# LSH attention and a gated mixing layer on one core: a new order of the instructions, one sign operation in the first batch, V's sums on two engines

## The chip, the core and the metric

The kernel runs on one core of a Trainium2 chip. The core has TensorE (PE, with PEld for its weight loads), VectorE (DVE), ScalarE (ACT), GpSimd (POOL) and SyncE (SP, which only issues DMAs here). Each engine runs its own list of instructions strictly in order and waits on semaphores for the others. The metric is the device time of one execution in microseconds (us), as a median over runs.

## What is computed

Four batches of eight heads, 768 tokens, head width 64. A 6-bit hash of each query and key (signs of a projection) masks the scores; softmax and PV follow. The heads' outputs, side by side, are the input `x` (768 x 512 per batch) of a mixing layer.

```
q_bits = (einsum(q, proj) > 0); k_bits = (einsum(k, proj) > 0)
mask = bucket(q_bits)[:, None] == bucket(k_bits)[None, :]
attn = softmax(where(mask, q @ k.T / 8, -1e9))        # per batch and head
x = concat over heads of attn @ v                     # 4 x 768 x 512
theta = x @ w_theta
y = w_tok_r @ (x * cos(theta)) + w_tok_i @ (x * sin(theta))
u = x + y
out = u + relu(u @ w_ch)
```

## The kernel before

Operands are split into a high and a low 16-bit float half, so that one product is three fp16 matmuls. Heads are loaded in pairs (`prep_qk`, `prep_v`), four pairs per batch.

**Queries and keys.** `bits` multiplies both heads' q and k by the projection into one PSUM bank `pb` of 128 rows; `sign` turns it on VectorE into the tile `rows`; DMAs (`assemble`) carry the halves `hl` and the `rows` into the matmul operand `qk` of the next head. For the very first head the pieces are copied by engines or DMAs one by one (`piece`). The 18 KB or 9 KB DMAs of `rows` and the 1.5 KB DMA of `row` stand in SyncE's one list with all loads.

**A head.** Score matmuls `sq` go to PSUM; VectorE takes row maxima (`mc`, then `mx`); TensorE transposes them (`pmx`), once per head and twice for the first head; VectorE makes `row` and `fl` of it, and DMAs put these into `qk` and into a flag tile `ft`. Then `st` matmuls (scores, transposed), exponentials `pf` on ScalarE, halves `p1` (ScalarE or GpSimd) and `p2` (GpSimd), and the PV matmuls `po`. Odd heads of batches 2 and 3 go another way (`bt`, `bm`, `late`).

**V.** `prep_v` scales V into halves (`vv`) and sums its six token blocks on GpSimd, in three instructions (`s1`, `s2`, in place in `vb`); a small matmul `pm` makes the mean of it.

**The mixing layer.** `ps_th` (theta), sines on ScalarE, the products `f` and halves `z` (VectorE, ScalarE, GpSimd), the token product `py`, then `s_u`, `ps_r`, and the store. The weights are prepared on the chip in the first 250 us (`wf_th`, `wf_ch`, `wf_t`), mostly on VectorE and ScalarE.

**The order.** Every step is an `op` with its alternatives by engine. The order of all ops, and the engine of each, is a table of numbers (`ORDER`, some 4,000 entries like `P2k`: letter = engine, rest = number of the op), and `SLOTS` says which of the rotating buffers each takes. `issue_all` writes them out in this order; so the table sets what each engine runs, one after the other.

**Beats.** 22 ops `beat` of two matmuls each on a constant flag tile keep TensorE busy in the first 22 us; their results are not used.

Of the kernel before, what the change touches and what calls it, by code (L numbers as in the profile page):

```python
# [11 lines left out]
F16 = mybir.dt.float16  # L12
F32 = mybir.dt.float32
# [19 lines left out]
def lsh_attention_moe_kernel(ctx: ExitStack, tc: tile.TileContext, q, k, v, proj, w_theta, w_tok_r, w_tok_i, w_ch, out):  # L33
# [6 lines left out]
    P = 128  # L40
# [27 lines left out]
    one33 = const.tile([P, 33], F16, name="one33")  # L68
    DVE.memset(one33, 1.0)
    ones1 = ones[:, :33]  # L70
# [8 lines left out]
    DVE.memset(fts[1], 1.0 / 1024)  # L79
# [25 lines left out]
    FREE = dict(ft=2, mc=2, hl=2, rows=2, sc=2, nat=2, vv=2, x=2, z0=1, z1=1, wx=1, wz=1, wf=1, xt=2, xd=2, vw=2, **BUFS)  # L105
# [28 lines left out]
    def on(e, dur, fn):  # L134
        return {e: (dur, fn)}
# [120 lines left out]
    def prep_weight(src, dst, nm, n, tag, stage, prio, step, by=1.0):  # L256
# [94 lines left out]
    def prep_v(b, hp, prio):  # L351
        t = {}
        full = t["full"] = [b == 0 and (hp, j) in FULL for j in range(2)]
        onpe = False
# [45 lines left out]
        def s1():  # L400
            POOL.tensor_tensor(t["vb"][:, :, 0:3], t["vb"][:, :, 0:3], t["vb"][:, :, 3:6], ALU.add)

        def s2():
            for n in (1, 2):
                POOL.tensor_tensor(t["vb"][:, :, 0], t["vb"][:, :, 0], t["vb"][:, :, n], ALU.add)

        def mean():
            t["pm"] = pm = bank(sm_, [33, 2, D], f"pm_{b}_{hp}")
            if onpe:
                first = True  # L410
                for j in range(2):
                    if full[j]:
                        for n in range(T):
                            mm(pm[:, j], ones1, t["vw"][j][:, n, :D], first, n == T - 1)
                            first = False
                if n_:
                    js = slice(lo_, lo_ + n_)
                    for n in range(2 * T):
                        c0 = 0 if n < T else W1
                        mm(pm[:, js], one33, t["vv"][:, js, n % T, c0 : c0 + D], first, n == 2 * T - 1)  # L420
                        first = False
            else:
                mm(pm, ones33, t["vb"][:, :, 0], True, True)

        def by(r):
            return 1.0 / S if onpe else sc[r]

        def mh():
            t["mh"] = ap_.tile([33, 2, D], F16, tag=f"mh{sv.idx}", bufs=1, name=f"mh_{b}_{hp}")
            ACT.activation(t["mh"], t["pm"], AF.Copy, scale=by(slice(0, 33)))  # L430
            ACT.activation(t["mt"][0:1, :, :D], t["pm"][0:1], AF.Copy, scale=by(slice(0, 1)))
# [13 lines left out]
        if not onpe:  # L445
            c = op("va1", prio, on("POOL", 970, s1), [c], [svb])
            c = op("va2", prio, on("POOL", 936, s2), [c], [svb])
        d = op("vmean", prio, on("PE", sum(700 if f_ else 380 for f_ in full) if onpe else 220, mean), [c], [svb, sv, sm_] + sw_)
# [184 lines left out]
    def maxima(h, n_, b, G, asm, own=False):  # L633
# [37 lines left out]
        for blk, (lo, hi) in {1: (4, 6), 0: (0, 4)}.items() if own else ((0, (0, T)),):  # L671
            def group(blk=blk, lo=lo, hi=hi):
# [3 lines left out]
                def small(nm_):  # L676
                    return ap_.tile([hi - lo, P], F16, tag=f"{nm_}{lo}_{hi}{smc.tag}", bufs=1, name=f"{nm_}_{nm}_{lo}")
# [638 lines left out]
FOURTHS = ()  # L1316
# [24 lines left out]
    "0000000000000000000000101012021202122001300010000011100100110020001010101103110002111111222033301001011033212201103003130110020311"  # L1341
    "1200111031011101010100011100101010111011132002201003031111030332022010111203032031100131203011010000000033000110011030011001111131"
    "1232103201211010303321211102001031332002021101001311120011101101130000100011130010101001131131100120011113030232020313200332101111"
    "3100311130011020310000000321011000101101111001010010123101000133201131021030012130032112103000103213000213012102320320111300010111"
    "2101010010000111101101010010011313010011213123201200211010113321023020130332112310011010023201031321101010003000021010000011000111"
    "0100012101013123200101323010102320120100113131332112200332010300201132120303201011011131011300111010100111001011013010032013213201"
    "0031000022313320300011101030103203201211102311321011022303000001200013111100011031102331133211000323021101000232102303111001000310"
    "0101200112321023031121110030000111110133010010111020112331111120012230311112300110200133200033032111212102233010121003000013312000"
# [212 lines left out]
```

## Time and profile before

| what | value |
|---|---|
| time, median of 3 runs (lowest, highest) | 689.69 us (689.42, 693.13) |
| the profiled execution: its own time | 687.36 us |
| the profiled execution: span, first to last instruction | 685.6 us |
| busy of the span: PE, DVE, ACT, POOL | 96%, 84%, 78%, 67% |
| granted TensorE clock | 0.999 |

Of the profiled execution 1.8 us lie around the span, and it is 2.3 us below the median of the runs. In the rows, L followed by a number is a line of the kernel before; most matmuls share the helper's line L82, so they are told apart by their tiles. A bracket at the end of a row is the idle time of the engine before it and what ended it.

### The profile page before, as it was taken

To read this page: it belongs to the slowest core of one execution; us is meant where nothing else is said; L and a number is where in the kernel's file an instruction comes from. 1 tells how busy PE (TensorE), PEld (TensorE's weight loads), DVE (VectorE), ACT (ScalarE), POOL (GpSimd) and SP (SyncE) were. 2 spreads that over 40 slices of the span, in tenths; PEclk is the share of its full clock that TensorE was granted. 3 is DMA by queue.
4 is the path that set the end of the run, shared out by engine and by line. 5 is a ranking of instruction groups with operands and counts; after the bars stand their busy time and mean duration, and the time that the engine had idled before them with its cause. 6 is when DMAs were issued, how large, how long until landed. Compare 5 with 4: busy or idle time off the path is not lost.

```text
span 685.6 us, 16806 instructions
## 1 busy us (share of the span) xinstructions
PE 659.5 (96%) x6257; PEld 389.7 (57%) x6257; DVE 579.1 (84%) x1236; ACT 535.8 (78%) x947; POOL 457.7 (67%) x453
## 2 busy tenths in 40 slices
PE   7899989899989999999999999999999999999997
PEld 2487776745544556656445565655645565644454
DVE  6999999999999999899988788889978778688121
ACT  5779989999977799999887889998984588873002
POOL 6838857378537668999568778978755898743012
PEclk9999999999999999999999999999999999999999
DMA  6564867677266452579537788989754685880113
GB/s 242 142 170 130 206 165 199 188 156 175 77 170 157 97 111 68 130 197 177 113 82 139 152 167 172 181 210 189 119 105 62 138 173 103 139 177 17 32 29 109
DMA packets 176985, 95.39 MB, mean 139 GB/s; under 512 B 149024, under 2 KB 166792, under 8 KB 176904
## 3 DMA queue, kind: packets, MB, share of 16 engines
q1 hardware_dynamic: 176760, 94.30, 61.4%
q8 instruction: 49, 0.80, 0.5%
q14 instruction: 32, 0.26, 0.2%
q10 hardware_dynamic: 144, 0.03, 0.0%
HBM read 32.53 MB, written 6.29 MB: 57 GB/s over the span
## 4 chain that ended last, share of the span: by engine, by line
PE 64%; DVE 23%; issue 5%; DMA 4%; ACT 2%; POOL 1%; SPq 0%; POOLq 0%; DVEq 0%; ACTq 0%
PE py L82 19%; PE po L82 13%; PE st L82 9%; PE ps_r L82 7%; DVE mc L660 6%; PE ps_th L82 6%; PE sq L82 4%; PE bt L82 4%; DVE f L1164 2%; DMA qk<-row 2%; DVE hl L498 1%; PE pb L82 1%; DVE z L1175 1%; DVE wf_t L244 1%; DVE wf_t L326 1%
## 5 line engine op out<-in xcount | busy, mean ns | idle before, releaser
L764 POOL TENSOR_TENSOR p<-pf,p 128x512 f16<-128x512 f32 x180 | 233.1, 1309 | 73.3 <-ACT p L758 62.9
L82 PE MATMUL py<-z,wtk 128*128 128x512 f16 (+1 forms) x900 | 206.6, 370 | 0.4 <-DVE mt L434 0.2
L660 DVE TENSOR_REDUCE mc<-sq 128x1 f32<-128x512 f32 (+1 forms) x216 | 143.2, 681 | 19.5 <-PE sq L82 18.3
L752 ACT ACTIVATE pf<-st 128x512 f32<-128x512 f32 x216 | 124.9, 592 | 22.0 <-PE st L82 17.5
L82 PEld LDWEIGHTS <-qk 108*128 108x128 f16 (+2 forms) x1056 | 96.1, 99 | 77.7 <-issue 17.7
L82 PEld LDWEIGHTS <-wtk 128*128 128x128 f16 x900 | 85.6, 97 | 89.8 <-issue 3.7
L82 PE MATMUL st<-qk 108*128 108x256 f16 (+1 forms) x576 | 124.9, 326 | 3.9 <-DMA qk<-row 2.3
L918 POOL TENSOR_TENSOR late<-pf,late 128x384 f16<-128x384 f32 x96 | 93.2, 985 | 25.2 <-ACT late L912 20.5
L82 PEld LDWEIGHTS <-p 128*128 128x128 f16 x2160 | 85.7, 97 | 21.5 <-issue 2.5
L758 ACT ACTIVATE p<-pf 128x512 f16<-128x512 f32 x148 | 90.7, 626 | 6.7 <-PE po L82 5.6
L82 PE MATMUL po<-vv,p 128*128 128x65 f16 (+1 forms) x2160 | 93.3, 193 | 0.1
L82 PE MATMUL sq<-qk 108*128 108x256 f16 (+1 forms) x288 | 78.5, 325 | 8.3 <-DVE mc L660 4.0
L904 ACT ACTIVATE pf<-bt,bm 128x384 f32<-128x384 f32 x96 | 60.7, 665 | 21.1 <-DVE bm L892 16.8
L82 PE MATMUL ps_th<-wth,t_x 128*128 128x512 f16 x288 | 68.2, 379 | 1.4 <-DVE z L1130 0.8
L82 PE MATMUL ps_r<-wch,t_u 128*128 128x512 f16 x276 | 68.9, 379 | 0.3 <-DVE wch L298 0.3
L876 DVE TENSOR_REDUCE bm<-bt 128x1 f32<-128x384 f32 x96 | 50.4, 549 | 11.2 <-PE bt L82 10.6
L1218 ACT ACTIVATE rl<-ps_r,qu 128x512 f32<-128x512 f32 x23 | 15.7, 683 | 46.8 <-PE ps_r L82 37.2
L82 PEld LDWEIGHTS <-t_x 128*128 128x128 f16 x288 | 27.4, 97 | 33.0 <-DMA t_x<-s_x 1.8
L1221 POOL TENSOR_TENSOR x<-rl,x 128x512 f32<-128x512 f32 (+1 forms) x9 | 12.0, 1328 | 48.2 <-DVE s_u L1020 32.7
L82 PE MATMUL bt<-qk 108*128 108x384 f16 x192 | 43.3, 327 | 0.0
L82 PEld LDWEIGHTS <-t_u 128*128 128x128 f16 x276 | 25.4, 97 | 26.8 <-issue 1.6
L1164 DVE SCALAR_TENSOR_TENSOR f<-x,zsc,z 128x512 f32<-128x512 f32 x48 | 38.8, 833 | 1.2 <-POOL z L1175 1.1
(177 smaller groups left out, 1084.0 us busy)
## 6 DMA issues: line engine op xcount, KB each, us to landing
qk<-hl SPq DMA_DIRECT2D x62, 192.0 KB
raw<-in_q_dram SPq DMA_DIRECT2D x16, 384.0 KB
raw<-in_k_dram SPq DMA_DIRECT2D x16, 384.0 KB
vb<-in_v_dram SPq DMA_DIRECT2D x16, 384.0 KB
qk<-hl SPq DMA_DIRECT2D x62, 96.0 KB
out_dram<-x SPq DMA_DIRECT2D x23, 256.0 KB
w_t<-in_moe_w_tok_r_dram SPq DMA_DIRECT2D x6, 768.0 KB
w_t<-in_moe_w_tok_i_dram SPq DMA_DIRECT2D x6, 768.0 KB
```

The source lines that it names most:

```text
L82: PE.matmul(out_, l, r, start=start, stop=stop, skip_group_check=True)
L244: return lambda: eng.tensor_tensor(t["f"][:, part], t["f"][:, part], t["sg"][:, part], ALU.mult)
L660: DVE.tensor_reduce(col()[:, cs], u["sq"], AX.X, ALU.max)
L752: ACT.activation(wide("pf", spf, F32), u["st"], AF.Exp, scale=1.0 / (UNIT * math.sqrt(D)))
L758: ACT.activation(o_, u["pf"], AF.Copy)
L764: return lambda: eng.tensor_tensor(wide("p2", sp2, F16), u["pf"], u["p1"], ALU.subtract)
L876: DVE.tensor_reduce(part(y), w["w"], AX.X, ALU.max)
L904: ACT.activation(w["f"], w["w"], AF.Exp, bias=part(4), scale=part(3))
L918: return lambda: eng.tensor_tensor(dst(1), w["f"], dst(0), ALU.subtract)
L1164: DVE.scalar_tensor_tensor(u["f"], tl[b][:, tt], zsc[:, b : b + 1], t["zw"][r][:, tt], ALU.mult, ALU.mult)
L1218: ACT.activation(v_["r"][:, ds_], r_["ps"][:, ds_], AF.Relu, scale=t["qu"][:, to : to + 1])
L1221: return lambda: eng.tensor_tensor(tl[b][:, to, ds_], v_["r"][:, ds_], tl[b][:, to, ds_], ALU.add)
```

## The change

1. `FOURTHS = (0,)`: in batch 0 `sign` is one instruction over 128 partitions instead of two over 64. Its result lies as 128 rows, so the DMAs that carry it to a head are four of 9 KB (`bits`) instead of two of 18 KB (`pairs`).
2. V's sums are one op with two alternatives: the three GpSimd instructions (`sums`), or one VectorE reduction over a strided view into a new tile `va` (`reduced`). The new table sends eight of the sixteen pairs to VectorE: pairs 1, 2, 3 of batch 1, 0, 1, 3 of batch 2, and 0, 1 of batch 3.
3. The beats read flag tile 1 instead of 0, and the two tiles' first fills change places. Two constants that only these or dead code used are gone; the weights' column totals are a one-pass bf16 matmul.
4. `SLOTS` and `ORDER` are new throughout: the row maxima rotate over three buffers instead of two, and all engines have another order.

```diff
-    DVE.memset(fts[0], 1.0 / 1024)
-    ones = const.tile([P, P], F32, name="ones")
-    DVE.memset(ones, 1.0)
+    DVE.memset(fts[1], 1.0 / 1024)
...
-            mm(tl["pw"], fts[0][:, :P], fts[0][:, :512], True, True)
+            mm(tl["pw"], fts[1][:, :P], fts[1][:, :512], True, True)
...
-            mm(u["pa"], ones, col, True, True)
+            mm(u["pa"], onesb, col.bitcast(BF16)[:, 1:2], True, True)
...
-        def s1():
+        def sums():
             POOL.tensor_tensor(t["vb"][:, :, 0:3], t["vb"][:, :, 0:3], t["vb"][:, :, 3:6], ALU.add)
-
-        def s2():
             for n in (1, 2):
                 POOL.tensor_tensor(t["vb"][:, :, 0], t["vb"][:, :, 0], t["vb"][:, :, n], ALU.add)
 
+        def reduced():
+            t["va"] = ap_.tile([P, 2, D], F32, tag="va" + svb.tag, bufs=1, name=f"va_{b}_{hp}")
+            DVE.tensor_reduce(t["va"], t["vb"].rearrange("p h t d -> p h d t"), AX.X, ALU.add)
...
-            c = op("va1", prio, on("POOL", 970, s1), [c], [svb])
-            c = op("va2", prio, on("POOL", 936, s2), [c], [svb])
+        c = op("va", prio, {"POOL": (1906, sums), "DVE": (860, reduced)}, [c], [svb])
...
-FOURTHS = ()
+FOURTHS = (0,)
...
-S66 S68 P0 So P3 Am S3c Pg S6t Pb A67 Dn P6k A69 D6a D6b Pj D6l P4 P2 D6c S6q A6o Pd G6n D6d D6e D6f Ph D6s S6r A6g Pi Pe D6p A6i P9 D6h Pf
```

What the new table does is seen in the instructions' order. VectorE at the start, up to the first row maxima; `sc` is the scale of the first pair, `rows` the signs, `qk` the first head's operand. Before:

```order
L516 RECIPROCAL sc_0_177<-sc_0_177 128x1
L543 TENSOR_SCALAR rows_0_191<-pb_0_181,pp 64x384 x2
L517 TENSOR_SCALAR sc_0_177<-sc_0_177 128x1
L518 TENSOR_SCALAR sc_0_177<-sc_0_177 128x1
L519 TENSOR_SCALAR sc_0_177<-sc_0_177 128x1
L520 TENSOR_SCALAR sc_0_177<-sc_0_177 128x2
L562 TENSOR_SCALAR qk_141<-raw_0_0_157,sc_0_177 32x768
L562 TENSOR_SCALAR qk_141<-raw_0_0_157,sc_0_177 64x768
L498 SCALAR_TENSOR_TENSOR hl_0_176<-raw_0_0_155,sc_0_177,hl_0_176 128x768
L498 SCALAR_TENSOR_TENSOR hl_0_176<-raw_0_0_157,sc_0_177,hl_0_176 128x768
L660 TENSOR_REDUCE mc_0_237<-sq_0_8_229 128x2
```

After:

```order
L497 TENSOR_SCALAR sc_0_175<-sc_0_175 128x1
L498 TENSOR_SCALAR sc_0_175<-sc_0_175 128x1
L499 TENSOR_SCALAR sc_0_175<-sc_0_175 128x1
L500 TENSOR_SCALAR sc_0_175<-sc_0_175 128x2
L523 TENSOR_SCALAR rows_0_195<-pb_0_177,pp 128x384
L542 TENSOR_SCALAR qk_137<-raw_0_0_153,sc_0_175 32x768
L540 COPY qk_137<-rows_0_195 12x384
L478 SCALAR_TENSOR_TENSOR hl_0_174<-raw_0_0_153,sc_0_175,hl_0_174 128x768
L190 TENSOR_SCALAR vsc<-pa_0_214 128x1
L191 TENSOR_SCALAR vinv<-vsc 128x1
L478 SCALAR_TENSOR_TENSOR hl_0_174<-raw_0_0_151,sc_0_175,hl_0_174 128x768
L640 TENSOR_REDUCE mc_0_238<-sq_0_6_231 128x1
```

The scale no longer stands behind the two sign instructions, one sign remains, and one of the copies of `rows` into the first head's operand is now here (three are on GpSimd, none is a DMA; two were DMAs).

ScalarE at the same place, from the squares of the raw q and k on. Before:

```order
L487 ACTIVATE hl_0_176,sc_0_177<-raw_0_0_157 128x768
L558 ACTIVATE qk_141<-rows_0_191 12x384
L492 ACTIVATE hl_0_176<-raw_0_0_155,sc_0_177 128x768
L492 ACTIVATE hl_0_176<-raw_0_0_157,sc_0_177 128x768
L558 ACTIVATE qk_141<-raw_0_0_155,sc_0_177 64x768
L380 ACTIVATE vv_121,vs_0_227<-vb_0_172 128x12x64
L391 ACTIVATE vw_137<-vb_0_172,vsc 128x6x64
```

After:

```order
L467 ACTIVATE hl_0_174,sc_0_175<-raw_0_0_153 128x768
L374 ACTIVATE vv_117,vs_0_183<-vb_0_158 128x12x64
L472 ACTIVATE hl_0_174<-raw_0_0_151,sc_0_175 128x768
L472 ACTIVATE hl_0_174<-raw_0_0_153,sc_0_175 128x768
L538 ACTIVATE qk_137<-raw_0_0_153,sc_0_175 64x768
L538 ACTIVATE qk_137<-raw_0_0_151,sc_0_175 64x768
L538 ACTIVATE qk_137<-hl_0_174 64x768 x2
L538 ACTIVATE qk_137<-hl_0_174 32x768
L385 ACTIVATE vw_133<-vb_0_158,vsc 128x6x64
```

V's squares moved ahead of the halves (V's load is now the third of SyncE's loads instead of the sixth), and of the first head's operand ScalarE makes five pieces (four of 64 rows, one of 32) instead of three (one of 64 and two smaller, one of them behind these rows).

VectorE in the middle of batch 1, where the first of its V sums stands now (`va`, pair 1 of batch 1); before, this place has no such row and GpSimd has the three instructions:

```order
L640 TENSOR_REDUCE mc_1_2_2574<-sq_1_2_1_2668 128x1
L1110 SCALAR_TENSOR_TENSOR z1_0_2286<-n_0_3_2673,mg_0_2279,ps_th0_3_2588 128x512
L401 TENSOR_REDUCE va_1_1_2698<-vb_1_1_2209 128x128
L640 TENSOR_REDUCE mc_1_2_2574<-sq_1_2_8_2677 128x2
L795 RECIPROCAL rc_1_0_0_2727<-po_1_0_0_2344 128x6
L640 TENSOR_REDUCE mc_1_2_2574<-sq_1_2_7_2691 128x1
```

It now stands between the row maxima of the head that follows.

Counted over the two orders: VectorE's instructions ahead of the maxima that the `pmx` of head 6 of batch 1 (the last of that batch) transposes.

| kind | before | after |
|---|---|---|
| sign, 64 partitions / 128 partitions | 18 / 0 | 10 / 4 |
| V's sums (`va`) | 0 | 3 |
| low half `z` by subtraction, 128x512 (L1175) | 8 | 6 |
| `wf_t` by sign (L244), `wf_ch` by sign, `wf_th` by sign (L250) | 10, 6, 1 | 9, 4, 2 |
| last sum `x<-rl,x` (L1221) | 1 | 0 |
| magnitude `z<-z` (L1133), cast to `z` (L1171) | 2, 2 | 1, 1 |
| `s_x<-x` high half (L1016) | 1 | 2 |
| first head: `qk<-raw` 64x768 (L562), copies into `qk` | 1, 0 | 0, 2 |

All other kinds of VectorE stand ahead of it as often as before (but for two fills). TensorE has 36 `po` matmuls more and two `st` matmuls of 512 columns fewer ahead of this `pmx`. ScalarE's list ahead of the same head's first `p1` has as many instructions as before but for one, partly of other kinds. SyncE has 92 entries instead of 81 ahead of the DMA of `row` for head 5 of batch 0, and 14 more DMAs for `rows` in all. Over the whole program all the work of TensorE is the same; GpSimd casts `p1` or `late` 16 times more and subtracts `z` four times more, and sums V eight times less.

## Rows read from the trace of the kernel before

**Rows 1.** The page: busy time by engine; then the span in 40 equal slices.
```profile
PE 659.5 (96%) x6257; PEld 389.7 (57%) x6257; DVE 579.1 (84%) x1236; ACT 535.8 (78%) x947; POOL 457.7 (67%) x453
PE   7899989899989999999999999999999999999997
DVE  6999999999999999899988788889978778688121
```
**Rows 2.** Windows: stretch in us, its length, busy time of PE, PEld, DVE, ACT, POOL.
```profile
0.00:20.00 20.00, 14.78 (x72) 5.76 (x72) 14.16 (x39) 11.01 (x19) 13.54 (x37) 1.00 0.67 225
20.00:80.20 60.20, 58.45 (x608) 42.22 (x605) 57.08 (x125) 51.13 (x98) 40.85 (x41) 1.00 0.58 155
80.20:180.00 99.80, 92.46 (x922) 61.46 (x921) 97.58 (x197) 93.18 (x159) 67.90 (x56) 1.00 0.70 172
180.00:272.80 92.80, 88.34 (x830) 49.61 (x829) 91.44 (x170) 77.36 (x144) 58.60 (x49) 1.00 0.49 118
272.80:480.00 207.20, 204.84 (x2113) 118.52 (x2112) 182.40 (x415) 185.57 (x339) 169.62 (x165) 1.00 0.76 158
480.00:660.00 180.00, 179.32 (x1574) 97.92 (x1572) 128.98 (x281) 113.31 (x185) 101.21 (x106) 1.00 0.54 101
660.00:685.60 25.60, 21.26 (x150) 14.18 (x147) 7.43 (x14) 4.25 (x8) 5.98 (x5) 0.98 0.33 93
```
**Rows 3.** Timeline of PE: `pmx` of head 5, batch 0, and of head 6, batch 1.
```profile
80.19 0.27 PE L684 MATMUL pmx<-ident,mx 128*6 128x128 f32 x1
...
272.84 0.27 PE L684 MATMUL pmx<-ident,mx 128*6 128x128 f32 x1
```
**Rows 4.** Timeline of all engines from 4 to 14 us: start, length, instruction.
```profile
4.12 0.84 ACT L487 ACTIVATE hl<-raw 128x768 f16<-128x768 f32 x1 [1.66 <-DMA raw<-in_q_dram]
5.83 0.19 ACT L487 ACTIVATION_READ_ACCUMULATOR hl<-raw 128x1 f32 x1
6.19 1.39 DVE L543 TENSOR_SCALAR rows<-pb,pp 64x384 f16<-64x384 f32 x2 [0.75 <-PE pb L82]
7.60 1.71 SPq L556 DMA_DIRECT2D qk<-rows  x2
7.61 0.21 DVE L517 TENSOR_SCALAR sc<-sc 128x1 f32<-128x1 f32 x1
7.96 0.50 POOL L560 COPY qk<-rows 12x384 f16<-12x384 f16 x1
8.23 0.25 DVE L520 TENSOR_SCALAR sc<-sc 128x2 f32<-128x2 f32 x1
8.52 1.76 ACT L492 ACTIVATE hl<-raw,sc 128x768 f16<-128x768 f32 x2 [1.10 <-DVE sc L520]
10.18 0.92 ACT L558 ACTIVATE qk<-raw,sc 64x768 f16<-64x768 f32 x1
12.51 0.87 ACT L380 ACTIVATE vv<-vb 128x768 f16<-128x768 f32 x1 [1.41 <-DMA vb<-in_v_dram]
12.98 0.59 PE L82 MATMUL sq<-qk 108*128 108x256 f16 x3 [2.90 <-DMA qk<-rows]
13.40 1.89 DVE L660 TENSOR_REDUCE mc<-sq 128x2 f32<-128x512 f32 x3 [1.78 <-PE sq L82]
```
**Rows 5.** Groups of DVE by form: line, shapes, count, busy us, mean ns, idle before.
```profile
L660 DVE TENSOR_REDUCE mc<-sq 128x1 f32<-128x512 f32 x144 | 96.9, 682 | 12.6 <-PE sq L82 11.7
L876 DVE TENSOR_REDUCE bm<-bt 128x1 f32<-128x384 f32 x96 | 50.4, 549 | 11.2 <-PE bt L82 10.6
L1175 DVE TENSOR_TENSOR z<-f,z 128x512 f16<-128x512 f32 x32 | 25.8, 824 | 2.4 <-ACT z L1169 1.8 <-POOL z L1171 0.5
L543 DVE TENSOR_SCALAR rows<-pb,pp 64x384 f16<-64x384 f32 x32 | 21.5, 672 | 1.0 <-PE pb L82 0.7
L1221 DVE TENSOR_TENSOR x<-rl,x 128x512 f32<-128x512 f32 x15 | 12.5, 834 | 1.0 <-ACT rl L1218 1.0
L244 DVE TENSOR_TENSOR wf_t<-wf_t 128x768 f32<-128x768 f32 x10 | 11.7, 1175 | 0.0
L231 DVE SCALAR_TENSOR_TENSOR wf_t<-w_t,wf_t 128x1536 uint32<-128x1536 uint32 x6 | 11.0, 1836 | 0.0
L227 DVE TENSOR_SCALAR wf_t<-w_t 128x1536 uint32<-128x1536 uint32 x6 | 5.7, 954 | 0.1
L1016 DVE TENSOR_SCALAR s_x<-x,zsc 128x512 f16<-128x512 f32 x8 | 5.1, 636 | 0.1
L1171 DVE CAST z<-f 128x512 f16<-128x512 f32 x9 | 4.0, 454 | 0.0
L1133 DVE TENSOR_SCALAR z<-z 128x512 uint32<-128x512 uint32 x8 | 4.0, 499 | 0.1
L250 DVE TENSOR_TENSOR wf_ch<-wf_ch,wg_ch 128x256 f32<-128x256 f32 x6 | 2.8, 462 | 0.0
L250 DVE TENSOR_TENSOR wf_th<-wf_th,wg_th 128x512 f32<-128x512 f32 x1 | 0.7, 669 | 0.0
L562 DVE TENSOR_SCALAR qk<-raw,sc 64x768 f16<-64x768 f32 x1 | 0.6, 612 | 0.0
```
**Rows 6.** Chain that ended last, in order of time: start, us, what.
```profile
38.60 0.87 PE st L82 x4
319.70 1.84 PE po L82 x60
```
**Rows 7.** Timeline of SyncE's issues before the `row` of three heads, batch 0.
```profile
41.81 0.36 SPq L481 DMA_DIRECT2D raw<-in_q_dram  x1
44.32 0.72 SPq L695 DMA_DIRECT2D qk<-row  x1
...
52.80 0.41 SPq L209 DMA_DIRECT2D w_ch<-in_moe_w_ch_dram  x1
55.27 0.72 SPq L695 DMA_DIRECT2D qk<-row  x1
...
77.66 2.89 SPq L321 DMA_TRANSPOSE wtk<-wf_t  x1
81.06 0.72 SPq L695 DMA_DIRECT2D qk<-row  x1
```
**Rows 8.** Timeline of PE: the first `st` of head 5, batch 0.
```profile
87.43 0.81 PE L82 MATMUL st<-qk 98*128 98x512 f16 x3 [1.88 <-DMA qk<-row]
```

More of the change, by code (lines that the diff above doesn't have):

```diff
@@ L62, in lsh_attention_moe_kernel @@
     fts = [const.tile([P, S], F16, name=f"ft{n}") for n in range(2)]
-    DVE.memset(fts[0], 1.0 / 1024)
-    ones = const.tile([P, P], F32, name="ones")
-    DVE.memset(ones, 1.0)
+    DVE.memset(fts[1], 1.0 / 1024)
     ones33 = const.tile([P, 33], F32, name="ones33")
     DVE.memset(ones33, 1.0 / S)
-    one33 = const.tile([P, 33], F16, name="one33")
-    DVE.memset(one33, 1.0)
-    ones1 = ones[:, :33]
     onesb = const.tile([P, P], BF16, name="onesb")
@@ L78, in lsh_attention_moe_kernel @@
         DVE.memset(pst[nm], 0.0)
-    DVE.memset(fts[1], 1.0 / 1024)
+    DVE.memset(fts[0], 1.0 / 1024)
     def mm(out_, l, r, start, stop):
@@ L104, in lsh_attention_moe_kernel @@
     phase = "0"
-    FREE = dict(ft=2, mc=2, hl=2, rows=2, sc=2, nat=2, vv=2, x=2, z0=1, z1=1, wx=1, wz=1, wf=1, xt=2, xd=2, vw=2, **BUFS)
+    FREE = dict(ft=2, mc=3, hl=2, rows=2, sc=2, nat=2, vv=2, x=2, z0=1, z1=1, wx=1, wz=1, wf=1, xt=2, xd=2, vw=2, **BUFS)
     def op(name, prio, alts, deps=(), slots=(), table=None):
@@ L398, in low @@
             DVE.scalar_tensor_tensor(t["vf"][:, hs_, W1 : W1 + D], src()[:, hs_], sc, t["vf"][:, hs_, :D], ALU.mult, ALU.subtract)
-        def s1():
+        def sums():
             POOL.tensor_tensor(t["vb"][:, :, 0:3], t["vb"][:, :, 0:3], t["vb"][:, :, 3:6], ALU.add)
-        def s2():
             for n in (1, 2):
                 POOL.tensor_tensor(t["vb"][:, :, 0], t["vb"][:, :, 0], t["vb"][:, :, n], ALU.add)
+        def reduced():
+            t["va"] = ap_.tile([P, 2, D], F32, tag="va" + svb.tag, bufs=1, name=f"va_{b}_{hp}")
+            DVE.tensor_reduce(t["va"], t["vb"].rearrange("p h t d -> p h d t"), AX.X, ALU.add)
         def mean():
             t["pm"] = pm = bank(sm_, [33, 2, D], f"pm_{b}_{hp}")
[L409 to L423, printed above, removed]
+            mm(pm, ones33, t["va"] if "va" in t else t["vb"][:, :, 0], True, True)
         def by(r):
-            return 1.0 / S if onpe else sc[r]
+            return sc[r]
         def mh():
-            t["mh"] = ap_.tile([33, 2, D], F16, tag=f"mh{sv.idx}", bufs=1, name=f"mh_{b}_{hp}")
+            t["mh"] = ap_.tile([33, 2, D], F16, tag="mh", bufs=1, name=f"mh_{b}_{hp}")
             ACT.activation(t["mh"], t["pm"], AF.Copy, scale=by(slice(0, 33)))
@@ L444, in prep_v @@
         c = last_
-        if not onpe:
-            c = op("va1", prio, on("POOL", 970, s1), [c], [svb])
-            c = op("va2", prio, on("POOL", 936, s2), [c], [svb])
-        d = op("vmean", prio, on("PE", sum(700 if f_ else 380 for f_ in full) if onpe else 220, mean), [c], [svb, sv, sm_] + sw_)
+        c = op("va", prio, {"POOL": (1906, sums), "DVE": (860, reduced)}, [c], [svb])
+        d = op("vmean", prio, on("PE", 220, mean), [c], [svb, sv, sm_] + sw_)
         f = op("vmh", prio, on("ACT", 500, mh), [d], [sm_, sv])
@@ L676, in small @@
                 def small(nm_):
-                    return ap_.tile([hi - lo, P], F16, tag=f"{nm_}{lo}_{hi}{smc.tag}", bufs=1, name=f"{nm_}_{nm}_{lo}")
+                    return ap_.tile([hi - lo, P], F16, tag=f"{nm_}{lo}{smc.tag}", bufs=1, name=f"{nm_}_{nm}_{lo}")
                 def both():
@@ L1345 @@
[L1345 to L1348, printed above, removed]
@@ L1497 @@
+P350 P35y A351 P361 A35z G352 D360 P362 P363 P364 S353 P365 A369 P366 P367 P368 D36a A36c G36d S36b S36e
 """
```

302 lines of the change are left out of this document (152 added, 150 removed).

## The prediction, made before the changed kernel ran

> **What bounds the kernel now.** I read the page first. PE is busy for 659.5 of 685.6 us, and its 40 slices are thin only in the first slice and in the first two fifths of the span [rows 1]. Only PE's idle time can change much, since all its matmuls remain. The windows say where that idle lies: 5.2 us in 0 to 20, 1.75 in 20 to 80.2, 7.3 in 80.2 to 180, 4.5 in 180 to 272.8, then 2.4 in the next 207 us, 0.7 in the next 180 and 4.3 in the tail [rows 2]. So 18.8 of the 26.1 us lie ahead of 272.8.
>
> Who is waited for there? From 80.2 to 272.8 DVE is busy for 97.58 + 91.44 = 189.0 of 192.6 us: DVE is the bound of that stretch, PE waits for it. From 20 to 80.2 PE is the bound (58.45 of 60.2). Behind 272.8 PE is within 1.2% of full until the tail. The two markers, the `pmx` of head 5 of batch 0 and of head 6 of batch 1, stand at 80.19 and 272.84 [rows 3]. My model of the time: **when the second marker comes, plus PE's remaining work, which stays as it is**, with the tail unchanged (the order of the last stores is the same in both tables). The second marker comes when DVE has done all that stands ahead of it: 14.16 + 57.08 + 97.58 + 91.44 = 260.3 us of work and 12.5 us of idle [rows 2].
>
> **DVE's work ahead of the second marker.** The counts are those of the table in the section on the change, the durations those of the groups [rows 5].
> - Sign: 18 instructions of 64 partitions become 10 and 4. An instruction's time goes by its 384 elements per partition, so one over 128 partitions is priced as one over 64: 4 x 0.672 = **-2.69**.
> - V's sums: three `va` more. The trace has no reduction of this form. Two contiguous reductions give a slope: 128 elements more cost 682 - 549 = 133 ns, 1.04 ns each, so one of 768 costs 682 + 256 x 1.04 = 0.95 us. Bounds: below, the 0.62 ns per element of L227 (954 ns for 1536, reading every second word), 0.48 us; above, the longest instruction of DVE, 1.84 us (L231). I take 0.95, the nearest row being a reduction: 3 x 0.95 = **+2.84**.
> - `z` by subtraction 2 fewer, -1.65; `wf_t` by sign -1.18; `wf_ch` two fewer and `wf_th` one more, -0.92 + 0.67; last sum -0.83; piece of `qk` -0.61; magnitude -0.50; cast -0.45; `s_x` +0.64. Two new copies into `qk` have no row on DVE; the nearest are GpSimd's 0.50 [rows 4] and DVE's 0.61 for a 64x768 piece: +0.6 for both, 0 to 1.2. Together **-4.2**.
>
> The fills (two more or fewer) stand in front of the first load's end and count nothing; if they did, some 0.3. Sum: -2.69 + 2.84 - 4.2 = **-4.1**. It becomes -3.7 if reductions are counted by their pitch back to back (three in 1.89, 0.63 each [rows 4]), since then `va` costs 0.90 and the others are shorter by similar shares. I take **-4**.
>
> PE has more ahead of the marker: 36 `po` at 1.84/60 = 0.031 us, +1.1, and two `st` fewer at 0.87/4 = 0.218, -0.4 [rows 6]: **+0.7** done early, which is taken from what remains behind it. PE's idle ahead of the marker therefore shrinks by 4.7 in all.
>
> **The start.** Before, the first `sq` waits 2.90 us for a DMA of `rows` and begins at 12.98, the first `mc` at 13.40 [rows 4]. The chain: two signs (6.19, 1.39 us) stand ahead of the scale's steps, which end at 8.48; ScalarE waits 1.10 for them; two DMAs of 1.71 in SyncE's list carry `rows`. After the change the scale's steps follow the read of the squares (6.02) at once. They ran from 7.61 to 8.48 and there is about as much ahead of 7.61 to do, so the scale ends near 7.1; the one sign (0.7) then ends near 7.8, three GpSimd copies (0.50 each) near 9.4. ScalarE makes the halves (1.76 for two) to 8.9 and two pieces (0.92 each) to 10.7. So the first `sq` comes near 10.7, about 2 us earlier (0 to 3). ScalarE now squares V between; if V's load landed later than 7 us, that would stall it, but V is now the third load.
>
> Are these 2 us worth anything? Between 20 and 80 PE is the bound, and DVE has 3.1 us idle there in which it waits for PE [rows 2]. An earlier start moves everything earlier, PE's idle in the first 20 us falls, and the first marker comes earlier; but DVE then still has all its work from 80 on. DVE's own work in the first 80 us falls by 2 too (signs, a piece), so I take DVE's idle ahead of the second marker to stay at 12.5, and allow -0.5 for ScalarE and queue effects that eat a little: **gain 4.7 - 0.5 = 4.2**.
>
> **Edits costed at nothing.** The beats on the other flag tile: PE has nothing else to do in those 20 us (5.2 idle [rows 2]); if their fill came late, they would start later by its length, under 1 us. The bf16 totals are two matmuls in the weights' preparation, under 0.1 us. Three `mc` buffers can only loosen a wait. The eight V sums moved off GpSimd free GpSimd, which is 67% busy [rows 1]; five of the eight stand on DVE behind the second marker, where DVE has 207.2 - 182.4 = 25 us to spare in one window [rows 2].
>
> **The rivals.**
> *More (D).* The earlier start counts too: DVE idles 2 us less ahead of the second marker. Gain 6.2, own time 681.2, median 683.5. For it: DVE's list is what bounds from 80 on. Against: it was PE that bound up to 80.
>
> *Nothing (A): ScalarE takes the bound.* In 80.2 to 180 ScalarE is busy for 93.18 of 99.80 us, DVE for 97.58 [rows 2]: ScalarE has only 4.4 us less to do there. For it: some 3 us of pieces and V's squares have moved into its start, and if it carries that lateness into this stretch, 4.4 - 3 = 1.4 of DVE's 4.7 us count, less with some waiting. Against: its own list up to the marker is as long as before. Gain 0 to 1, median 689 (688 to 690.5).
>
> *Little (B): the strided reduction costs twice as much.* `va` reads six words 256 bytes apart for each sum. At the upper bound of 1.84 us the three cost 5.5 instead of 2.8, gain 1.5, median 688.2. Against: L227 with every second word shows no penalty (0.62 ns per element) [rows 5], but its step is 8 bytes. The Trainium skill, page "SBUF — State Buffer", section "Door 1: The DMA port swizzle (why `[64,N]` ≈ `[32,N]`)", speaks against the change here: SBUF has 16-byte lines, and each access that crosses to a new line pays a penalty. By that rule L227, two hits to a line, would be free, as the trace has it, and `va`, a new line with every word, would not; no row of this trace has such a step.
>
> *Slower (C): SyncE's list.* Four DMAs of `rows` instead of two, and 14 more in all, stand in the one list that also puts `row` into `qk`; two take 1.71 to issue [rows 4], so 14 are 12 us in batch 0, with 11 more entries ahead of the `row` of head 5. Puts now follow the previous issue by 44.32 - 42.17 = 2.1 and 55.27 - 53.21 = 2.1 us, so SyncE waits there; but for head 5 by 81.06 - 80.55 = 0.5 only, behind a 2.89 us transposition [rows 7], and the `st` of that head waits 1.88 for it [rows 8]. If two DMAs more (1.7) land in front of a `row`, that head's `st` is late by up to 1.7. With seven heads: 7 x 1.7 - 4.2 = +7.7 (697.4); with four, +2.6 (692.3). It decides from three heads on (5.1 against 4.2). Against: two of the three heads looked at have 2.1 us of slack.
>
> **How the numbers follow.** The forecast: span 685.6 - 4.2 = 681.4; with 1.8 around it, own time 683.2; the profiled execution lay 2.33 below the median, so the median is **685.5**. Its own range is 683.5 to 687.5: `va` from 0.48 to 1.84 moves the gain from 5.6 to 1.5, the start from 0 to 3 moves it by about a half to each side. Chances: forecast 0.52, D 0.09, A 0.17, B 0.10, C 0.12. A measurement of this kernel can tell some 0.5%, 3.4 us, from no change; the forecast lies at 4.2, so 0.37 of its 0.52 count as faster and 0.15 as the same. Faster: 0.37 + 0.09 = 0.46. Same: 0.15 + A 0.17 + B 0.10 = 0.42. Slower: C, 0.12. The range from 681.5 to 690.5 takes in D, A, B and the forecast's bounds and leaves out C and the far ends.
>
> **What would show it.** The first `sq` near 10.7 us, without a wait on a DMA; `va` at 0.95 us each, 1.8 would be B; `pmx` of head 6 of batch 1 near 268.6, with DVE still idle for about 12.5 us ahead of it (10.5 would be D); the same share of PE behind it. ScalarE idle for under 3 us from 80 to 180 would be A. `st` waits on `row` above 1.9 us in several heads of batch 0 would be C. My forecast is wrong at its base if the time behind the second marker changes: then PE's remaining work was not the constant I take it for, or a wait moved there.

## The result, and the profile after

The changed kernel took 699.65 us (median of four runs, 698.38 to 701.10), the kernel before 690.70 in its four: the ratio is 1.0125 (95% interval 1.0086 to 1.0163). The forecast was 685.5, with a range of 681.5 to 690.5. The profiled execution spans 696.6 us; its own time is 698.38. Each ratio is to executions of the kernel before taken beside that kernel, and leaves out those with a disturbed clock, so it can differ from the quotient of the medians.

The page of the changed kernel: busy time, then two rows of the 40 slices (PE, and the clock that TensorE was granted).

```profile
PE 669.0 (96%) x6255; PEld 394.7 (57%) x6255; DVE 588.3 (84%) x1230; ACT 534.1 (77%) x938; POOL 450.5 (65%) x447
PE   7899999879999999999999999999999999999997
...
PEclk9999969989999999999999999999999999999999
```

PE is busy for 9.5 us more than before [rows 1], for the same matmuls. Slices 6 and 9 have a clock of 0.6 and 0.8. Over the whole profiled execution the mean granted clock is 0.984; the other three runs had 0.977 to 0.980, so they lost more. Four windows of the changed kernel show both places, the pause and what followed (columns as in [rows 2]: the clock is the third number from the end).

```profile
85.50:88.50 3.00, 0.17 (x2) 0.09 (x1) 0.86 (x2) 0.65 (x2) 2.94 (x3) 1.00 1.10 136
...
90.40:103.90 13.50, 13.50 (x57) 10.18 (x56) 7.68 (x12) 7.64 (x13) 4.61 (x4) 0.50 0.37 117
...
145.90:148.40 2.50, 0.14 (x5) 0.04 (x2) 2.50 (x4) 0.98 (x5) 1.45 (x1) 0.97 1.15 190
148.40:155.00 6.60, 6.06 (x30) 3.34 (x30) 6.60 (x10) 5.81 (x10) 5.91 (x4) 0.50 0.72 150
```

Twice PE pauses for nearly 3 us, and at the pause's end or soon after it the clock is at the lower level (1.2 GHz, a granted clock of 0.50), for at least 13.5 and 6.6 us. PE's timeline names what each pause waited for; its first and last row are the two markers of the prediction.

```profile
79.92 0.27 PE L664 MATMUL pmx<-ident,mx 128*6 128x128 f32 x1
...
88.41 0.38 PE L77 MATMUL st<-qk 98*128 98x512 f16 x1 [2.83 <-DMA qk<-row]
...
148.94 0.37 PE L77 MATMUL sq<-qk 108*128 108x256 f16 x1 [2.90 <-DVE mc L640]
...
284.13 0.27 PE L664 MATMUL pmx<-ident,mx 128*6 128x128 f32 x1
```

The first wait stood in the kernel before too, 1.88 us [rows 8], without a fall. SyncE's timeline shows why it grew.

```profile
71.81 3.72 SPq L595 DMA_DIRECT2D qk<-rows  x4
...
77.74 0.38 SPq L204 DMA_DIRECT2D w_t<-in_moe_w_tok_r_dram  x1
78.18 0.41 SPq L204 DMA_DIRECT2D w_t<-in_moe_w_tok_i_dram  x1
78.69 2.96 SPq L316 DMA_TRANSPOSE wtk<-wf_t  x1
81.75 0.71 SPq L675 DMA_DIRECT2D qk<-row  x1
```

Four DMAs of `rows` take 3.72 us of issue where two took 1.71 [rows 4]. The transposition is issued at 78.69 instead of 77.66 and `row` at 81.75 instead of 81.06 [rows 7], though the marker came 0.27 us earlier than before.

The three windows cut at the markers:

```profile
0.00:79.92 79.92, 73.93 (x679) 48.22 (x680) 71.28 (x159) 66.06 (x119) 51.94 (x70) 1.00 0.57 167
79.92:284.13 204.21, 190.50 (x1785) 117.06 (x1782) 189.37 (x362) 170.36 (x300) 128.49 (x108) 0.95 0.60 142
284.13:696.60 412.47, 404.61 (x3802) 229.43 (x3798) 327.65 (x710) 297.68 (x520) 270.12 (x271) 1.00 0.64 129
```

Behind the second marker lie 412.5 us, before 685.6 - 272.84 = 412.8. So the whole loss lies ahead of it, between the two markers: 204.2 us instead of 192.65.

### The profile page after: what moved, and what is told of

Read it like the earlier page. It is cut to its first block, busy times and chain, and to the rows that moved or that the text cites. A ratio compares the mean times of both kernels' runs of the same rounds, so it can differ in the third digit from the quotient of the medians.

```text
span 696.6 us, 16742 instructions
## 1 busy us (share of the span) xinstructions
PE 669.0 (96%) x6255; PEld 394.7 (57%) x6255; DVE 588.3 (84%) x1230; ACT 534.1 (77%) x938; POOL 450.5 (65%) x447
## 4 chain that ended last, share of the span: by engine, by line
PE 65%; DVE 19%; DMA 6%; issue 4%; POOL 2%; ACT 2%; SPq 1%; POOLq 0%; DVEq 0%; ACTq 0%
PE py L77 22%; PE po L77 12%; PE st L77 9%; PE ps_th L77 6%; PE ps_r L77 6%; DVE mc L640 5%; PE sq L77 5%; PE bt L77 3%; DMA late<-late 2%; DMA t_x<-s_x 1%; DVE wf_t L321 1%; POOL late L898 1%; DMA qk<-row 1%; DVE hl L478 1%; DVE f L1144 1%
## 5 line engine op out<-in xcount | busy, mean ns | idle before, releaser
L744 POOL TENSOR_TENSOR p<-pf,p 128x512 f16<-128x512 f32 x180 | 230.2, 1294 | 72.3 <-ACT p L738 60.7
L77 PE MATMUL st<-qk 108*128 108x256 f16 (+1 forms) x576 | 129.0, 335 | 6.1 <-DMA qk<-row 3.0
L898 POOL TENSOR_TENSOR late<-pf,late 128x384 f16<-128x384 f32 x96 | 94.7, 999 | 23.8 <-ACT late L892 21.0
L738 ACT ACTIVATE p<-pf 128x512 f16<-128x512 f32 x142 | 86.9, 625 | 9.8 <-PE po L77 8.2
L77 PE MATMUL po<-vv,p 128*128 128x65 f16 (+1 forms) x2160 | 91.7, 193 | 0.0
L77 PE MATMUL sq<-qk 108*128 108x256 f16 (+1 forms) x288 | 81.1, 331 | 10.6 <-DVE mc L640 7.5
L884 ACT ACTIVATE pf<-bt,bm 128x384 f32<-128x384 f32 x96 | 61.0, 665 | 27.0 <-DVE bm L872 15.6
L77 PE MATMUL ps_th<-wth,t_x 128*128 128x512 f16 x288 | 69.9, 384 | 1.3 <-DMA t_x<-s_x 1.3
L1201 POOL TENSOR_TENSOR x<-rl,x 128x512 f32<-128x512 f32 (+1 forms) x8 | 9.5, 1192 | 60.2 <-ACT rl L1198 60.2
L77 PEld LDWEIGHTS po<-vw,pf 128*128 128x128 f32 x288 | 39.9, 206 | 4.2 <-ACT p L738 0.9
L1144 DVE SCALAR_TENSOR_TENSOR f<-x,zsc,z 128x512 f32<-128x512 f32 x48 | 41.2, 877 | 0.9 <-ACT z L1133 0.6
```

Source lines behind the costliest of these rows:

```text
L77: PE.matmul(out_, l, r, start=start, stop=stop, skip_group_check=True)
L738: ACT.activation(o_, u["pf"], AF.Copy)
L744: return lambda: eng.tensor_tensor(wide("p2", sp2, F16), u["pf"], u["p1"], ALU.subtract)
L884: ACT.activation(w["f"], w["w"], AF.Exp, bias=part(4), scale=part(3))
L898: return lambda: eng.tensor_tensor(dst(1), w["f"], dst(0), ALU.subtract)
L1144: DVE.scalar_tensor_tensor(u["f"], tl[b][:, tt], zsc[:, b : b + 1], t["zw"][r][:, tt], ALU.mult, ALU.mult)
```

## The experiments

Theory T: SyncE's list is longer by the DMAs of `rows` (four to a head instead of two); the pause at head 5 passes from 1.9 to 2.8 us; the clock falls behind it, and behind a second pause that the new order of VectorE makes. Rivals are named with each run.

**1. The pause filled.** In the first chunk of head 5's `scores`:

```diff
+                    for _ in range(12 if (nm, c) == ("0_5_0", 0) else 0):
+                        mm(u["st"][:, :P], ident, ident, True, True)
```

> The changed kernel with 12 unused matmuls of 128x128 in f32 (some 2.6 us of TensorE, none of whose results is read) ahead of the first st of head 5, batch 0, where TensorE waited 2.83 us for the row DMA at 85.6 us; everything else, the order included, is the changed kernel's. Theory T (TensorE's pause of 2.83 us is followed by the fall of its granted clock to 0.50 from 90.4 to 103.9 us, and 13.5 us at half speed cost 6.7): no fall there, time 693 us, between 691.5 and 694.5; st itself starts no earlier than 88. Rival R (the new order is slower by itself, VectorE's 10 us of extra busy time being the reason, and the clock only marks a pause that costs 1 us): 699 to 700, whatever the clock does.

Measured: 690.2 us, ratio to before 0.9986 (0.9964 to 1.0008). The windows of this kernel, from the filler on:

```profile
85.00:88.60 3.60, 3.60 (x34) 3.24 (x31) 1.51 (x2) 1.29 (x3) 3.52 (x4) 1.00 1.18 152
88.60:104.00 15.40, 15.29 (x131) 12.06 (x129) 14.51 (x29) 13.69 (x25) 8.50 (x8) 1.00 0.55 155
```

The clock stays at 1.00 and 15.4 us hold 131 matmul records, where 13.5 held 57. Useless work took 9.5 us off the median, 6.75 of which T expected; that it is more fits the clock of the changed kernel's other runs, which lay below that of its profiled one. R falls: the order was the same, and `st` itself began at 88.04, hardly earlier than 88.41. The second pause (2.91 us) and its fall are still in this profile:

```profile
142.00:148.70 6.70, 6.20 (x31) 3.37 (x31) 6.70 (x10) 5.76 (x10) 6.06 (x4) 0.50 0.80 139
```

**2. Two signs, two DMAs**: `FOURTHS = ()` in the changed kernel.

> The changed kernel with the sign of batch 0 done as before, in two instructions of 64 partitions, its rows carried by two DMAs of 18 KB instead of four of 9 KB; the new order, V's sums and all else as changed. Theory T (the 14 extra issues push SyncE's list back, the loads of w_t and the row of head 5 are issued about 1 us later, and the pause passes from 1.9 to 2.8 us): the row lands 1 to 3 us earlier, the pause is under 1.9 us, no fall of the clock at 90 us, time about 693.5 (692 to 695). Rival S (the sign's saving on VectorE is a gain that is kept): 0.7 us more per pair on VectorE, so 700 to 702.

Measured: 688.99 us, ratio 0.9957 (0.9917 to 0.9996). The time is below T's, S is excluded. No `st` of head 5 waits, but not for the reason written down: `row` was put later than in the changed kernel (83.33), since the marker came at 82.60 instead of 79.92, and PE had other work until it landed. The second sign accounts for only 0.67 of these 2.7 us; three weight instructions of VectorE in front of the marker took longer too (0.98, 0.88 and 0.28 us), why is open. The second pause stays at 2.84 us, with a fall of little over 3.2:

```profile
85.50:103.90 18.40, 18.25 (x189) 14.66 (x187) 18.04 (x35) 17.05 (x32) 15.08 (x12) 1.00 0.66 163
...
141.50:144.70 3.20, 3.20 (x14) 1.62 (x11) 3.20 (x3) 3.20 (x6) 3.20 (x3) 0.50 0.91 180
```

**3. The first part alone**: `FOURTHS = (0,)` in the kernel before.

> The kernel before, in its own order, with the sign of batch 0 as one instruction over 128 partitions and four DMAs of 9 KB for its rows (the change's first part alone). Theory T: SyncE's list runs up to 2 us later ahead of head 5, its row lands later than 87.4 us, TensorE's pause grows from 1.9 to 2.8 or more and the clock falls for some 13 us: 695 to 698. Rival S: VectorE saves four signs ahead of the marker, 687 to 690. If the pause grows and the clock stays at 1.0, T is wrong on the clock.

Measured: 699.2 us, ratio 1.0081 (1.0035 to 1.0128). PE's row of the wait, and the window behind it:

```profile
92.75 1.44 PE L82 MATMUL st<-qk 98*128 98x512 f16 x3 [3.63 <-DMA qk<-row]
```

```profile
92.70:109.80 17.10, 17.05 (x91) 12.26 (x91) 9.34 (x14) 9.37 (x14) 4.74 (x6) 0.52 0.44 123
```

So this part by itself makes the old order slower, with the same wait and a long fall, at a time above T's 695 to 698. The clock may not be all of it: the three runs at 0.994 to 0.998 still took 694.5 to 695.6, the 20 of the kernel before beside them at such clocks 689.5 to 694.7.

**4. The transposition behind the row**: `S12` moved behind `Shi` in `ORDER`.

> The changed kernel with one entry of SyncE's list moved: the transposing DMA of wf_t (2.96 us to issue) that stands ahead of head 5's row goes behind that row and its flags. Theory T1 (the row is late because this transposition stands ahead of it): row put at 80.7 instead of 81.75 and landing 2 to 3 us earlier, pause under 1 us, no fall at 90 us, 692 to 694. Theory T2 (the row is late because the 1.5 MB of w_t stand ahead of it in the DMA queues; st came 10.7 us after their first issue in both kernels): row lands at most 1 us earlier, pause about 1.9, and the clock then stays or falls as a pause of that length decides.

Measured: 693.75 us, ratio 1.0007 (0.9972 to 1.0041). At head 5 T1 holds: PE is busy for 4.85 of the 5 us from 85 on, `row` being put at 80.34. But two transpositions (4.02 us) now stand in front of head 6, and the pause moved there:

```profile
100.29 0.59 PE L77 MATMUL st<-qk 98*128 98x512 f16 x1 [2.23 <-DMA qk<-row]
```

```profile
85.00:90.00 5.00, 4.85 (x39) 3.63 (x37) 4.89 (x10) 4.19 (x9) 4.92 (x4) 1.00 0.90 200
...
99.20:109.80 10.60, 9.51 (x50) 6.37 (x50) 4.30 (x9) 6.09 (x14) 3.52 (x3) 0.52 0.61 189
142.50:145.30 2.80, 0.01 (x1) 0.01 (x1) 2.80 (x5) 1.30 (x5) 1.19 (x1) 1.00 0.90 162
145.30:150.00 4.70, 3.79 (x33) 2.31 (x33) 4.70 (x5) 4.70 (x9) 4.57 (x3) 1.00 0.92 191
```

The last two rows are the second pause, 2.83 us again, and what follows it: here no fall.

**5. The maxima forward**: `Dpm` and `Dq0` (two `vmax`) moved ahead of `D4n` (`wf_ch`).

> The changed kernel with two entries of VectorE's list moved: in batch 1 the two row maxima for which sq waited 2.90 us at 146.0 us go ahead of the weights' instruction (wf_ch, 1.37 us) and the s_x subtraction that stood in front of them. Theory T (that pause is followed by the second fall of the clock, 148.4 to 155.0 us, 6.7 us at half speed): pause about 1 us, no second fall, the first fall stays: 694 to 696.5. Rival: VectorE is the bound there, so what is moved behind the maxima is late in their place and the gain is under 1 us: 698.5 to 700.

The cause of that pause in the changed kernel, VectorE's timeline:

```profile
146.25 1.37 DVE L226 SCALAR_TENSOR_TENSOR wf_ch<-w_ch,wf_ch 128x256 uint32<-128x256 uint32 x1
147.55 0.74 DVE L1000 SCALAR_TENSOR_TENSOR s_x<-x,zsc,s_x 128x512 f16<-128x512 f32 x1
148.21 1.27 DVE L640 TENSOR_REDUCE mc<-sq 128x1 f32<-128x512 f32 x2
```

Measured: 699.05 us (689.63 to 700.66), ratio 1.0042 (0.9994 to 1.0089), so a miss for T by the median, which lies in the rival's 698.5 to 700. The profile (span 692.8) shows what T says, a pause of 0.95 and no second fall, but the first fall came after a pause of 1.78 us, shorter than the one of [rows 8] that had none:

```profile
87.48 0.38 PE L77 MATMUL st<-qk 98*128 98x512 f16 x1 [1.78 <-DMA qk<-row]
```

```profile
89.60:103.40 13.80, 13.80 (x61) 10.48 (x61) 7.91 (x12) 7.86 (x13) 4.81 (x5) 0.52 0.36 114
```

The one run without any fall (clock 1.0) took 689.63. The runs with a clock of 0.978 to 0.983 took 699 to 700.7; only the profiled run shows where its clock fell, so which places those are in the others is open.

**6. Both pauses shortened**: edits 2 and 5 together.

> The changed kernel with both pauses shortened: the sign of batch 0 in two instructions with two DMAs, and the two row maxima of batch 1 moved forward. Theory T: no fall of the clock in the first 600 us, clock 0.998 or more; 3 us less than with the two signs alone (688.99), so 684.5 to 687.5, clear of the kernel before. Rival: the rest of the new order is no better than the old one, 689 to 691.

Measured: 687.17 us (686.73 to 687.69), ratio 0.9897 (0.9831 to 0.9964): faster than both kernels; its slowest run is below the fastest of the 25 of the kernel before that it is compared with (688.61). The clock is whole up to the second marker:

```profile
0.00:82.61 82.61, 74.94 (x680) 48.11 (x681) 75.78 (x163) 65.88 (x119) 51.25 (x72) 1.00 0.61 183
82.61:273.12 190.51, 180.98 (x1780) 111.52 (x1781) 186.19 (x362) 169.71 (x300) 128.52 (x107) 1.00 0.60 143
```

**7. V's sums on GpSimd** in kernel 6: the eight `va` entries changed from `D` to `G`.

> As the kernel with both pauses shortened, and the eight sums of V that the change gives to VectorE (1.50 us each) are done by GpSimd again, at the same places of the order (three instructions, some 2.2 us). If VectorE bounds up to the end of batch 1, its three sums there are worth up to 4.5 us: 681.5 to 684. If they lie in VectorE's pauses, no change from that kernel. If GpSimd's p2 halves wait for the sums in its list, slower by 1 to 4 us.

Measured: 696.49 us, ratio 1.0027 (0.9991 to 1.0063), at a clock of 0.995 to 1.0: slower than kernel 6 by 9.3 us, more than the third case's 4. One short fall is in the profile, behind a pause of 1.24 us at a place where kernel 6 has the same pause and no fall:

```profile
141.50:144.90 3.40, 3.32 (x10) 1.43 (x10) 3.40 (x7) 3.40 (x7) 3.40 (x3) 0.50 0.90 182
```

Half of its 3.4 us, 1.7, is what it can cost. The second marker is at 277.06 (3.9 later); behind it lie 417.6 us instead of 412.8, and there PE waits for the sums themselves, 2.1 us in two places. One of them:

```profile
453.39 0.41 PE L77 MATMUL pm<-vb,ones 128*33 128x128 f32 x2 [1.59 <-POOL vb L397]
```

What makes up the rest of the 9.3 is open.

**8. The kernel before, its pause filled** (8 such matmuls, in its own `scores`).

> The kernel before with 8 unused matmuls of 128x128 in f32 (1.7 us, results not read) ahead of the first st of head 5, batch 0, where TensorE paused 1.88 us. Of 31 runs of the kernel before on this chip, six took 698 us or more at a clock of 0.977 to 0.986. Theory T (those runs are ones in which this pause was a little longer and the clock fell): none of the runs over 696 us, the others as before, 689.5 to 691. Rival (they come from elsewhere): one run in five stays at 698 or more.

Measured: 691.98 us (689.01 to 695.56), ratio 0.998 (0.994 to 1.0021); no run above 696, as T has it, but the others are spread wider than it said. The profile shows a fall at the other pause, that of the first `sq`, and a second one of 3.3 us behind a pause of 2.15 us, in front of the `pmx` at 196.4. The first:

```profile
10.30:13.10 2.80, 0.00 (x0) 0.01 (x1) 1.45 (x2) 1.39 (x3) 2.15 (x2) 0.89 0.44 124
12.20:19.80 7.60, 6.68 (x21) 2.73 (x22) 4.48 (x11) 3.71 (x8) 3.23 (x6) 0.55 0.38 121
```

**9. One sign, no pauses**: edits 1 and 5 together.

> The changed kernel, its one sign operation and four DMAs kept, with both pauses taken away: the 12 unused matmuls ahead of the first st of head 5, and the two row maxima of batch 1 moved forward. Theory T: no fall of the clock. If the one sign instruction then saves what it was costed at (four times 0.67 us of VectorE ahead of the end of batch 1), 684.5 to 686.5, below the 687.17 of the kernel with two signs. If SyncE's list is the price of it even without a fall, 688 to 690.

Measured: 688.48 us (684.28 to 690.01, four runs), ratio 0.9857 (0.9785 to 0.9929). No fall up to the second marker. The low ratio is partly the clock of the kernel before: its four runs beside this one at 0.997 or more took 686.18 to 690.17, and from those 688.48 is not clear. Whether one sign or two is better (687.17 above) these spreads don't tell. The windows show what the new order does when both pauses are gone:

```profile
0.00:79.31 79.31, 74.88 (x679) 48.30 (x680) 71.24 (x159) 65.73 (x119) 52.14 (x70) 1.00 0.58 173
79.31:274.46 195.15, 184.01 (x1807) 113.99 (x1805) 187.62 (x362) 169.68 (x300) 127.57 (x108) 1.00 0.63 147
```

**10. Dense sums** in kernel 6 (other words are summed, so eight means are not those wanted):

```diff
-            DVE.tensor_reduce(t["va"], t["vb"].rearrange("p h t d -> p h d t"), AX.X, ALU.add)
+            DVE.tensor_reduce(t["va"].rearrange("p h d -> p (h d)"), t["vb"].rearrange("p h t d -> p (h t d)").rearrange("p (x s) -> p x s", s=T), AX.X, ALU.add)
```

> The kernel with two signs and the maxima moved forward (687.17), in which each V sum of VectorE adds six words that lie side by side instead of six that are 256 bytes apart: as many words read and sums written, the result is another one (the means of those eight pairs are wrong). If the step between the words is what makes va 1.50 us instead of the 0.95 that was costed, va takes about 0.95, and if VectorE bounds there, 1.6 us of the time go: 685 to 686. If the 128 results of six words each cost as such, va stays at 1.5 and the time at 687.

The group of the changed kernel, then that of this one:

```profile
L401 DVE TENSOR_REDUCE va<-vb 128x128 f32<-128x768 f32 x8 | 12.0, 1500 | 0.0
```

```profile
L401 DVE TENSOR_REDUCE va<-vb 128x128 f32<-128x768 f32 x8 | 7.5, 935 | 0.0
```

The view with a step of 256 bytes costs 0.565 us of 1.50. The time, 686.88 (684.63 to 690.56), doesn't tell whether that is felt.

**11. Two signs, four DMAs**: in `pairs`, for batch 0, one DMA for each half of `rows`.

> The changed kernel in its own order, with the sign of batch 0 in two instructions as before but the rows still carried by four DMAs of 9 KB. Theory T (the number of entries in SyncE's list is what costs, not the sign operation): pause at head 5 of 2.8 us or more, clock about 0.98, 698 to 702. Rival (one instruction over 128 partitions delays the rows or VectorE itself): as with two signs and two DMAs, 687 to 691.

Measured: 694.5 us (691.28 to 696.91), ratio 1.0027 (0.9993 to 1.0061), between the two answers. Against run 2 only the DMAs differ: they cost 5.5 us by the medians, 4.8 by the ratios. The pause turns up at head 6, with a fall behind it; a second fall, of 6.8 us, begins at 145.2, while PE is busy and before its pause of 1.41 us there:

```profile
103.77 0.38 PE L77 MATMUL st<-qk 98*128 98x512 f16 x1 [2.16 <-DMA qk<-row]
```

```profile
104.30:111.90 7.60, 7.60 (x45) 5.31 (x44) 2.57 (x6) 5.09 (x12) 2.91 (x2) 0.55 0.59 213
```

**12. Both pauses of the kernel before filled**: 8, and 13 more ahead of its very first `sq`.

> The kernel before with unused matmuls of 128x128 in f32 at both of its long pauses: 13 (2.8 us) ahead of the very first sq, where TensorE paused 2.90 us at 10.1, and 8 (1.7 us) ahead of the first st of head 5. With the second pause alone filled, one profiled run showed a fall of the clock from 12.2 to 19.8 us, right behind the first pause, and ended at 695.6. Theory T (the kernel before loses its clock in some runs at the one place or the other): all runs at a clock of 0.996 or more, none above 693, median 688 to 690. Rival (the spread of the kernel before comes from elsewhere): runs up to 695 remain, median 692 as with the one pause filled.

Measured: 693.68 us (690.66 to 697.35), ratio 1.0027 (0.9995 to 1.006). T's forecast failed: six runs are above 693, and the median is not below that of the kernel before (691.77). The rival's runs up to 695 are nearer. But a third pause was left, 2.14 us in front of the `pmx` at 195.2, and in this profile the clock falls behind it:

```profile
196.80:200.10 3.30, 3.30 (x34) 2.12 (x32) 2.98 (x6) 2.56 (x5) 0.81 (x1) 0.50 0.42 89
```

And the time does go with the clock. In the 82 runs of the kernel before that stand beside the twelve experiments, the 31 at 0.997 or more have a median of 690.7 (686.2 to 693.8), the 33 at 0.990 to 0.996 one of 692.7 (689.5 to 697.3), the 18 below 0.990 one of 698.8 (697.2 to 706.8). So the kernel before has such losses too, in some of its executions; the changed kernel had them in all four. What spreads the runs of one clock (691.5 to 693.9 at 0.998 here) stays open.

## Why the prediction was wrong

*What bounds, and the model.* The time as "when the second marker comes, plus PE's remaining work" held: behind the marker 412.5 us, forecast 412.8 - 0.7 = 412.1. (With that remainder the marker belonged at 681.4 - 412.1 = 269.3; the 268.6 among the signs leaves out the 0.7.) The marker came at 284.13, so the prediction failed ahead of it.

*The start.* First `sq` at 10.91, forecast 10.7. The first marker came earlier, as forecast, but only by 0.27 us: ahead of it PE had 73.93 us of work instead of 73.23, and idled for 6.0 us instead of 7.0. VectorE's work up to it did not fall by 2 us, as the prediction had it; it was 71.28 against 71.24.

*VectorE's work ahead of the marker*, forecast 256.3 us, was 71.28 + 189.37 = 260.65, where before had 260.3: a term mis-sized by 4.35. `va` took 1.50 us instead of 0.95, three times: 1.65. That is nearer to rival B's 1.84 than to the price I took from contiguous rows. The Trainium skill's rule ("SBUF — State Buffer", "Door 1: The DMA port swizzle (why `[64,N]` ≈ `[32,N]`)": a penalty for each access that crosses to a new line) pointed the right way. Run 10 shows the size for this step, 0.565 us. The other 2.7 is the balance of instructions that took longer or shorter than the rows of before: the high half of `wf_ch` stood at 1.37 us in the place shown, and at 0.41 in run 9, with the maxima ahead of it. Why is open. In run 9 the whole sum is 71.24 + 187.62 = 258.9, still 2.6 over the forecast.

*VectorE's idle time ahead of it*, forecast to stay near 12.5, was 284.13 - 260.65 = 23.5. This is the step that failed: 11 us more, where the prediction kept the idle of before and put TensorE's clock at nothing. Some 8.3 of the 11 lie between the `pmx` of head 5 and the second one behind it, where the first pause and fall are; before, then after (the third busy time is VectorE's, 25.24 of 26.50 and 23.43 of 33.02):

```profile
80.19:106.69 26.50, 23.90 (x247) 18.11 (x246) 25.24 (x52) 23.29 (x43) 19.16 (x18) 1.00 0.80 193
79.92:112.94 33.02, 29.92 (x244) 22.71 (x241) 23.43 (x50) 21.99 (x42) 18.31 (x17) 0.79 0.64 160
```

In the second fall VectorE is busy for all of 6.60 us, so that fall is not idle time of VectorE. What the pauses and falls cost together is seen in run 9, which has neither of the two: its second marker is at 274.46, 9.7 us earlier. PE's own busy time says nearly the same: it rose ahead of the marker by 264.4 - 254.1 = 10.3, of which 0.7 is work moved forward. The Trainium skill, page "TensorE: Matmul & The Clock Gate", section "Terms", puts the penalty of throttled time at about that time by one less the ratio of the clocks. By it an estimate for the 13.5 + 6.6 = 20.1 us is 10.0, and the trace has 9.6.

The clock is not the whole miss. At a full clock run 9 still has the marker 5.2 us behind the forecast of 269.3: 2.6 of that is VectorE's work, the rest its idle, 15.6 where 12.5 and an allowance of 0.5 stood. Even then the marker is later than the 272.84 of before, so the forecast gain did not come.

*The rivals.* C named the right list, the right DMAs, the right head and the right wait, and gave each such wait its own length, 1.7 us, so that three heads were needed. One head was enough, because a pause of PE can cost several times its length afterwards. Whether the 0.95 us that this pause grew by made the fall is not shown: in run 5 a pause of 1.78 us, shorter than the 1.88 of before, was followed by one. I looked at the clock only to note that it was 0.999, and never asked what it would do. Runs 1, 2 and 6 show the price of the pauses, runs 3 and 11 that the DMAs bring such a pause as the first. The second pause stands in no rival: it comes of VectorE's new order, where a weight instruction and an `s_x` stand in front of two row maxima (run 5). A and D were not met: ScalarE was not what was waited for, and the startup did not count.

*Costed at nothing.* The sums moved off GpSimd: in the new order run 7 gives them 9.3 us, up to 1.7 of it a fall of the clock. GpSimd's share of busy time (67%) said nothing of its place in that order. No run takes the beats, the bf16 totals or the third `mc` buffer by itself.

## What to carry to other kernels

Price a wait of TensorE in two parts, its own length and what the clock may do behind it; that a wait of 2 us is harmless in one execution does not make it so in the next. A split of two DMAs into four (1.71 us of issue, then 3.72) delays everything behind them in the queue, so look for the put that already follows its predecessor at once. When a change of the order moves the time by more than its waits, look at the row of the granted clock first, and fill the pause with useless matmuls: here two lines of code told the clock from the order (run 1).

## What the runs showed of the hardware

A pause's length alone did not decide whether the clock fell, nor for how long. Falls came behind pauses of 1.24 (runs 7 and 10), 1.78, 1.87 (runs 3 and 10), 2.14 (runs 3 and 12), 2.15 and 2.82 (run 8), 2.16, 2.23, 2.83, 2.90 and 3.63 us; none behind 1.88, 2.14 and 2.90 in the kernel before, behind 2.83 in run 4 and behind 1.24 in run 6. Behind a pause of some 2.85 us at one and the same place of the order, the stretch at 0.50 was some 6.6, 3.2 and 0 us long (changed kernel, runs 2 and 4). A busy PE did not end a fall at once: in the changed kernel it was busy for 13.50 of 13.50 us at 0.50. A reduction over words 256 bytes apart took 1.50 us, over adjoining ones 0.935, for 768 words in and 128 out.
